# Two-chunk second and last tiles in a fused linear-attention and MLP kernel, with full-decay opening masks and a last block in halves

## The chip, the cores and the metric

The kernel runs on one core of one Trainium2 chip. The metric is the device time of one execution in microseconds (us). Profiles are of one execution; their span runs from the first to the last recorded instruction and is about 1.8 us shorter than the device time of that same execution. All runs used here are fast ones.

In the profile's lines PE is TensorE, PEld its weight loads, ACT ScalarE, DVE VectorE, POOL GpSimd and SPq the queue of SyncE. A line of a timeline gives start, duration, engine, line of the kernel, operation, what it writes `<-` what it reads, and in brackets the idle time before it with what ended it.

## The reference

Linear attention with a decay per head, then an MLP with ELU.

```python
# q, k, v: (batch 4, heads 8, seq 768, head_dim 64), lam: one decay per head
for b in range(nb):                               # blocks of the sequence
    intra = einsum('bhic,bhjc->bhij', qb, kb) * Dmask      # lam ** (i - j), causal
    intra = einsum('bhij,bhjd->bhid', intra, vb)
    inter = einsum('bhid,bhde->bhie', qb * lam_pow, kv_state)
    out[block] = intra + inter
    kv_state = lam_block * kv_state + einsum('bhsd,bhse->bhde', kb * rev_pow, vb)
x = out, as (3072 tokens, 512)
h = x @ w_in                                      # 512 x 2048
g = where(h > 0, h, exp(min(h, 0)) - 1)           # ELU
y = g @ w_out                                     # 2048 x 512
```

## The kernel before

The attention works in 24 chunks of 128 tokens (6 along the sequence for each of 4 batches, numbered with the batch fastest). The MLP works in six tiles of four chunks. A tile has 16 slices of d_ff. For a slice TensorE makes four 128x512 matmuls (`psH`, the *hidden* matmuls); ScalarE makes `e = Exp` and `r = Relu` of it; VectorE makes the ELU, `g = min(e - 1, r)`. In slices 3, 5 and 7 of tile 0 VectorE does it in two instructions instead, `m = min(e - 1, 0)` and `g = max(m, psH)`, to spare ScalarE. The *output* matmuls (`psM`) are 16 per chunk.

```python
TS = [4, 4, 4, 4, 4, 4]                           # chunks per tile
...
def mm1(t, n, alt=False):                         # one slice of a tile
    ...                                           # 4 matmuls 128x512 into pH
    nc.scalar.activation(e[:], pH[:], AF.Exp)
    if alt:
        return e, None, pH
    nc.scalar.activation(r[:], pH[:], AF.Relu)

def elu(t, n, e, r, pH):
    if r is None:
        nc.vector.tensor_scalar(out=m[:], in0=e[:], scalar1=-1.0, scalar2=0.0, op0=ALU.add, op1=ALU.min)
        nc.vector.tensor_tensor(out=gt[t][:, n, :], in0=m[:], in1=pH[:], op=ALU.max)
        return
    nc.vector.scalar_tensor_tensor(out=gt[t][:, n, :], in0=e[:], scalar=-1.0, in1=r[:], op0=ALU.add, op1=ALU.min)
```

The attention of a pair of chunks is a *visit* with three slots in the hand-written order: `s0` transposes q and k, `s1` makes the scores `psS` and their masked copy `P`, `s2` makes the outputs `psO`, the MLP input `xt` and the next state. For the pairs in the table `XT` the two transposes are DMA transposes, issued at the slot in the table; for the others TensorE transposes and ScalarE copies.

```python
XT = {12: (1, 10), 14: (2, 2), 16: (2, 10), ...}  # pair: (tile, slice) of the DMA transposes
def visit(g, s0, s1, s2):
    if g in XT:
        at(XT[g], att_xT, g)                      # nc.sync.dma_start_transpose, q then k
    else:
        at(s0, att_T, g, 2, "q"); at(s0, att_T, g, 2, "k")      # TensorE
        at(s0, att_Te, g, 2, "q", "a"); at(s0, att_Te, g, 2, "k", "a")  # ScalarE copies
    at(s0, att_kd, g, 2, "v")                     # kd = k * decay, VectorE
    at(s1, att_S, g); at(s1, att_S, g + 1); at(s1, att_mask, g); at(s1, att_mask, g + 1)
    at(s2, att_O, g, 2); at(s2, att_U, g); at(s2, att_X, g, 2); ...
for g, vs in [..., (8, ((1, 0), (1, 2), (1, 5))), (10, ((1, 8), (1, 10), (1, 13))), (12, ((2, 0), (2, 2), (2, 5))), ...]:
    visit(g, *vs)
```

All loads of q, k, v and the weights are issued by GpSimd, in a hand-written order that also holds GpSimd's two products `kd` (chunks 0 and 1, chunks 2 and 3).

Of the kernel before, what the change touches and what calls it, by code (L numbers as in the profile page):

```python
# [7 lines left out]
FP32 = mybir.dt.float32  # L8
# [7 lines left out]
def kernel(  # L16
# [10 lines left out]
    nc = tc.nc  # L27
# [9 lines left out]
    TS = [4, 4, 4, 4, 4, 4]  # L37
# [75 lines left out]
    def zero_states(e):  # L113
        for j in range(B // 2):
            for i in range(2):
                e.memset(st[j][i][:], 0.0)

    LOADS = [(0, 1, 'q'), (0, 1, 'k'), (0, 1, 'v'), (1, 1, 'q'), (1, 1, 'k'), (1, 1, 'v'), (2, 1, 'q'), (2, 1, 'k'), (3, 1, 'q'), (3, 1, 'k'), ('wi', 0), (2, 1, 'v'), ('wi', 1), (3, 1, 'v'), ('wi', 2), ('wi', 3), ('wi', 4), ('wi', 5), ('kd', 0), ('wi', 6), ('kd', 2), ('wo', 0), (4, 2), ('wo', 1), (6, 2), ('wo', 2), ('wo', 3), (8, 2), (10, 2), (12, 2), (14, 2), (16, 2), (18, 2), (20, 2), (22, 2)]
# [23 lines left out]
    rel = cpool.tile([128, 128], FP32, name="rel")  # L142
    nc.vector.tensor_copy(rel[:], rel_i[:])
    nc.vector.tensor_copy(pos[:, 0:1], rel[:, 0:1])
# [3 lines left out]
    nc.vector.tensor_scalar_add(pos[:, 1:2], pos[:, 0:1], float(L))  # L148
    nc.vector.tensor_scalar(
        out=causT[:], in0=rel[:], scalar1=0.0, scalar2=None, op0=ALU.is_ge  # L150
    )
    nc.vector.tensor_scalar(
        out=row[:], in0=rel[:], scalar1=pos[:, 0:1], scalar2=None, op0=ALU.subtract
    )

    dn = cpool.tile([128, H], FP32, name="dn")
    nc.scalar.activation(dn[:], loglam[:], AF.Exp, scale=pos[:, 0:1])
    mask = cpool.tile([128, 2, HP, 128], FP32, name="mask")
    for hh in range(2):
        nc.vector.tensor_tensor(  # L160
            out=mask[:, hh],
            in0=causT[:].unsqueeze(1).broadcast_to([128, HP, 128]),
            in1=dn[:, hh::2].unsqueeze(2).broadcast_to([128, HP, 128]),
            op=ALU.mult,
        )

    zero_states(nc.vector)
# [5 lines left out]
    def late_consts():  # L173
        for hh in range(2):
            r = slice(hh * 64, (hh + 1) * 64)
            nc.scalar.copy(loglam_p[r, :], loglam[r, hh::2])
        for hp in range(HP):
            nc.scalar.activation(
                qs[:, hp, :], row[:], AF.Exp, scale=loglam_p[:, hp : hp + 1]
            )  # L180
        nc.scalar.activation(ks[:], loglam[:], AF.Exp, scale=pos[:, 1:2])
        nc.scalar.activation(up_p[:], loglam_p[:], AF.Exp, scale=float(L))
# [75 lines left out]
    def att_mask(g, parts=1):  # L258
        P = asb.tile([128, 2, HP, 128], FP16, tag="P", name=f"P{g}", bufs=3)
        s = pS.pop(g)  # L260
        w = HP // parts
        for i in range(parts):
            c = slice(i * w, (i + 1) * w)
            nc.vector.tensor_tensor(  # L264
                out=P[:, :, c], in0=s[:, :, c], in1=mask[:, :, c], op=ALU.mult
            )
        Pt[g] = P
# [25 lines left out]
    def att_X(g, n, parts=1):  # L293
        t, i = where[g]
        if i == 0:
            xt[t] = asb.tile([128, HP, TS[t] * L], FP16, tag="xt", name=f"xt{t}")
        po = pS.pop(("O", g))
        w = HP // parts
        for j in range(parts):
            c = slice(j * w, (j + 1) * w)  # L300
            nc.vector.tensor_tensor(  # L301
                out=xt[t][:, c, i * L : (i + n) * L].rearrange("p h (n l) -> p n h l", n=n),
                in0=po[:, :, c],
                in1=qs[:, c].unsqueeze(1).broadcast_to([128, n, w, 128]),
                op=ALU.mult,
            )
# [70 lines left out]
    def mm1(t, n, alt=False):  # L377
        MT = TS[t] * L
        if (t, n) not in pH_of:
            mm1_mm(t, n, 0, MT, "M" if t == 0 and n % 2 == 1 and n < 8 else "H")  # L380
        pH = pH_of.pop((t, n))
        e = msb.tile([128, MT], FP32, tag="e", bufs=3, name=f"e{t}_{n}")
        nc.scalar.activation(e[:], pH[:], AF.Exp)  # L383
        if alt:
            return e, None, pH
        r = msb.tile([128, MT], FP16, tag="r", bufs=3, name=f"r{t}_{n}")
        nc.scalar.activation(r[:], pH[:], AF.Relu)  # L387
        return e, r, pH

    def elu(t, n, e, r, pH):  # L390
        if r is None:
            m = msb.tile([128, TS[t] * L], FP16, tag="r", bufs=3, name=f"m{t}_{n}")
            nc.vector.tensor_scalar(
                out=m[:], in0=e[:], scalar1=-1.0, scalar2=0.0, op0=ALU.add, op1=ALU.min
            )
            nc.vector.tensor_tensor(out=gt[t][:, n, :], in0=m[:], in1=pH[:], op=ALU.max)  # L396
            return
        nc.vector.scalar_tensor_tensor(  # L398
            out=gt[t][:, n, :], in0=e[:], scalar=-1.0, in1=r[:], op0=ALU.add, op1=ALU.min
        )  # L400

    def mm2(t, i, n, tag="M"):
        if n == 0:
            psM[t, i] = ps.tile([128, DM], FP32, tag=tag, bufs=2, name=f"psM{t}_{i}")
        pm = psM[t, i]
        nc.tensor.matmul(  # L406
            pm[:], lhsT=gt[t][:, n, i * L : (i + 1) * L],
            rhs=wo_t[wo_at[n][0]][:, wo_at[n][1], :], start=(n == 0), stop=(n == NF - 1),
        )
        if n < NF - 1:  # L410
            return
        c, b = divmod(T0[t] + i, B)
        t0 = b * S + c * L
        o = msb.tile([128, DM], FP32, tag="osb", bufs=3, name=f"osb{t}_{i}")
        last = T0[t] + i == NG - 1
        if last:
            hw = DM // 2
            nc.vector.tensor_copy(o[:, 0:hw], pm[:, 0:hw])
            nc.sync.dma_start(out=out[t0 : t0 + L, 0:hw], in_=o[:, 0:hw])
            nc.scalar.copy(o[:, hw:], pm[:, hw:])  # L420
            nc.scalar.dma_start(out=out[t0 : t0 + L, hw:], in_=o[:, hw:])
        else:
            if i % 2:
                nc.vector.tensor_copy(o[:], pm[:])  # L424
            else:
                nc.scalar.copy(o[:], pm[:])  # L426
            nc.sync.dma_start(out=out[t0 : t0 + L, :], in_=o[:])
        psM.pop((t, i))

    def warm(k):  # L430
        if k <= 0:
            return
        pw = ps.tile([128, 4, 128], FP32, tag="M", bufs=2, name=f"psW{len(warms)}")
        warms.append(pw)
        for _ in range(k):
            nc.tensor.matmul(
                pw[:], lhsT=ident16[:], rhs=any16, start=True, stop=True
            )
# [16 lines left out]
    def op_Te(c, w):  # L455
        att_Te(c, 1, w, "a")

    W = [5, 2, 3, 0, 1, 0, 0, 1, 1, 0, 0]
    warm(W[0])
    op_T(0, "q")  # L460
    op_Te(0, "q")
    warm(W[1])
    op_T(0, "k")
    op_Te(0, "k")
    late_consts()
# [11 lines left out]
    warm(W[5])  # L477
    op_T(2, "q")
    op_Te(2, "q")
    att_S(1)  # L480
    att_mask(1, 2)
    warm(W[6])
    op_T(2, "k")
    op_Te(2, "k")
    op_T(3, "q")
    op_Te(3, "q")
    warm(W[7])
    att_S(2)
    att_mask(2, 2)
    op_T(3, "k")  # L490
    op_Te(3, "k")
    att_O(1, 1, "M")
    att_X(1, 1)
    warm(W[8])
    att_S(3)
    att_O(2, 1, "M")
    att_X(2, 1)
    att_mask(3, 2)
    warm(W[9])
    for n in range(1):  # L500
        mm1_mm(0, n, 0, 3 * L, "HM"[n % 2])
    att_O(3, 1)
    att_X(3, 1, 2)
    warm(W[10])
    for n in range(1, 3):
        mm1_mm(0, n, 0, 3 * L, "HM"[n % 2])
    for n in range(3):
        mm1_mm(0, n, 3 * L, 4 * L)

    run_loads(LOADS[17:27])  # L510
# [8 lines left out]
    XT = {12: (1, 10), 14: (2, 2), 16: (2, 10), 18: (3, 2), 20: (3, 10), 22: (4, 2)}  # L519

    def visit(g, s0, s1, s2):
        if g in XT:
            at(XT[g], att_xT, g)
        else:
            at(s0, att_T, g, 2, "q")
            at(s0, att_T, g, 2, "k")
            at(s0, att_Te, g, 2, "q", "a")
            at(s0, att_Te, g, 2, "k", "a")
        at(s0, att_kd, g, 2, "p" if g in () else "v")
        at(s1, att_S, g)  # L530
        at(s1, att_S, g + 1)
        at(s1, att_mask, g)
        at(s1, att_mask, g + 1)
        at(s2, att_O, g, 2)
        at(s2, att_U, g)
        at(s2, att_X, g, 2)
        at(s2, att_st, g)
        at(s2, att_tmp, g + B)

    for g, vs in [(4, (('A', 11), ('A', 13), ('A', 15))), (6, (('B', 6), ('B', 9), ('B', 12))), (8, ((1, 0), (1, 2), (1, 5))), (10, ((1, 8), (1, 10), (1, 13))), (12, ((2, 0), (2, 2), (2, 5))), (14, ((2, 8), (2, 10), (2, 13))), (16, ((3, 0), (3, 2), (3, 5))), (18, ((3, 8), (3, 10), (3, 13))), (20, ((4, 0), (4, 2), (4, 5))), (22, ((4, 8), (4, 10), (4, 13)))]:  # L540
        visit(g, *vs)
    for s, a, b in [(('A', 14), 27, 28), (('A', 15), 28, 29), (('B', 11), 29, 30), (('B', 13), 30, 31), ((1, 1), 31, 32), ((1, 5), 32, 33), ((1, 9), 33, 34), ((1, 13), 34, 35)]:
        at(s, run_loads, LOADS[a:b])
# [43 lines left out]
```

## Time and profile before

Time before: 220.01 us, median of 3 runs (219.97 to 220.41); span 218.6 us.

The first lines are from the profile's page: busy time of the engines, then TensorE's busy share and clock in 40 slices of the span, the queue of the software-issued loads, and the two costliest groups.

```profile
PE 204.8 (94%) x1593; PEld 100.3 (46%) x1593; DVE 150.3 (69%) x190; ACT 126.8 (58%) x234; POOL 79.2 (36%) x76
...
PE   5979789899998999999999999999999999999992
...
PEclk9999999999999999999999999999999999999999
...
q0 software_dynamic: 80208, 13.63, 89.2%
...
L372 PE MATMUL psH<-xt,wi 128*128 128x512 f16 (+2 forms) x396 | 98.0, 372 | 2.8 <-DVE g L396 1.1
L406 PE MATMUL psM<-wo,g 128*128 128x512 f16 x384 | 97.6, 380 | 0.0
```

TensorE is the limit: it is busy 94% of the span, and after the thirteenth slice of its row (from 71 us) there are only nines until the last. The busy time by stage, in the windows view, shows where it is not.

```profile
core 0: us, PE busy (x) PEld busy (x) DVE busy (x) ACT busy (x) POOL busy (x), PEclk, DMA share, GB/s
0.00:18.00 18.00, 12.92 (x111) 6.24 (x113) 11.49 (x23) 9.49 (x20) 17.00 (x24) 1.00 1.66 121
18.00:42.00 24.00, 20.63 (x199) 10.62 (x199) 19.66 (x23) 18.85 (x35) 22.26 (x20) 1.00 1.78 183
42.00:54.00 12.00, 11.84 (x121) 6.42 (x122) 10.73 (x12) 2.67 (x4) 9.80 (x9) 1.00 2.05 173
54.00:74.00 20.00, 19.11 (x179) 9.98 (x178) 18.21 (x20) 17.14 (x31) 15.20 (x13) 1.00 2.16 175
74.00:80.00 6.00, 6.00 (x71) 3.22 (x70) 5.94 (x10) 4.35 (x10) 3.38 (x3) 1.00 2.89 154
```

From 42 to 54 us TensorE makes output matmuls of tile 0 alone, and ScalarE is busy only 2.67 of 12 us: that is what the change wants to use. Because the ends of pipelined matmuls are modelled, I also count a *stall* as the time from one matmul's start to the next, less its streaming time (columns at 216 ns for 512; small ones at their traced pace). Counted so, the stages lose 9.1, 5.1, 0.6, 1.8 and 0.1 us (the last one 74 to 78 us), and the whole span 18.3 us.

The two issued between 55 and 84 us, however, are behind the loads; the view of the tile `kT` in that window says so.

### The profile page before, as it was taken

The numbers are of one execution on the slowest core, as the hardware profiler recorded it, in microseconds if no ns is written. First come the engines' busy times: TensorE is split into PE (matmuls) and PEld (weight loads), VectorE is DVE, ScalarE is ACT, GpSimd is POOL, SyncE is SP. The second block draws the span as 40 slices with busy tenths as digits, with TensorE's granted clock in tenths as the row PEclk, the third lists the DMA queues.
The fourth block names the chain that finished last, engine by engine and source line by source line (L and its number), as shares of the span: only waits on it lengthen the run. The fifth ranks groups of instructions, "written<-read, shape, count | busy, mean of one in ns | idle before, by whom it ended". The sixth has DMA issues, their size and how long they took to land.

```text
span 218.6 us, 3968 instructions
## 1 busy us (share of the span) xinstructions
PE 204.8 (94%) x1593; PEld 100.3 (46%) x1593; DVE 150.3 (69%) x190; ACT 126.8 (58%) x234; POOL 79.2 (36%) x76
## 2 busy tenths in 40 slices
PE   5979789899998999999999999999999999999992
PEld 1444334455554544544544544545445444444440
DVE  2775879997799999897887786776666544534000
ACT  5643899332978876456466566456456566674110
POOL 8999979699958478210300000000000000000000
PEclk9999999999999999999999999999999999999999
DMA  6999999999999999999143052061011011110221
GB/s 42 144 158 190 206 163 182 183 176 157 200 184 154 157 149 167 144 166 184 39 96 97 3 116 76 2 138 58 0 48 51 0 48 48 49 51 0 96 96 49
DMA packets 96643, 23.33 MB, mean 107 GB/s; under 512 B 88816, under 2 KB 93680, under 8 KB 96624
## 3 DMA queue, kind: packets, MB, share of 16 engines
q0 software_dynamic: 80208, 13.63, 89.2%
q1 hardware_dynamic: 16272, 9.31, 18.1%
q8 instruction: 12, 0.20, 0.4%
q10 hardware_dynamic: 144, 0.13, 0.2%
q14 instruction: 7, 0.06, 0.1%
HBM read 27.27 MB, written 6.29 MB: 153 GB/s over the span
## 4 chain that ended last, share of the span: by engine, by line
PE 71%; DVE 13%; POOL 5%; ACT 5%; issue 2%; DMA 2%; DVEq 0%; POOLq 0%; ACTq 0%
PE psM L406 34%; PE psH L372 30%; DVE g L398 5%; DVE P L264 3%; PE psO L277 2%; DMA vn<-in_v_dram 2%; ACT e L383 2%; ACT r L387 2%; DVE kd L239 2%; POOL qn L72 2%; POOL kn L72 2%; PE psO L285 2%; PE psS L252 2%; POOL vn L72 1%; DVE st L355 1%
## 5 line engine op out<-in xcount | busy, mean ns | idle before, releaser
L372 PE MATMUL psH<-xt,wi 128*128 128x512 f16 (+2 forms) x396 | 98.0, 372 | 2.8 <-DVE g L396 1.1
L406 PE MATMUL psM<-wo,g 128*128 128x512 f16 x384 | 97.6, 380 | 0.0
L398 DVE SCALAR_TENSOR_TENSOR g<-e,r 128x512 f16<-128x512 f32 x93 | 71.3, 780 | 37.5 <-ACT r L387 37.3
L383 ACT ACTIVATE e<-psH 128x512 f32<-128x512 f32 x96 | 57.6, 604 | 59.3 <-PE psH L372 56.8
L372 PEld LDWEIGHTS <-wi 128*128 128x128 f16 x396 | 37.8, 98 | 47.6 <-issue 5.2
L387 ACT ACTIVATE r<-psH 128x512 f16<-128x512 f32 x93 | 55.7, 599 | 0.0
L406 PEld LDWEIGHTS <-g 128*128 128x128 f16 x384 | 36.2, 98 | 41.9
L264 DVE TENSOR_TENSOR P<-psS,mask 128x1024 f16<-128x1024 f32 (+1 forms) x28 | 28.7, 1066 | 3.1 <-PE psS L252 3.0
L336 POOL TENSOR_TENSOR tmp<-st,up_p 64x512 f32<-64x512 f16 x16 | 21.6, 1347 | 21.2 <-DVE st L355 20.3
L301 DVE TENSOR_TENSOR xt<-psO,qs 128x1024 f16<-128x1024 f32 (+2 forms) x15 | 15.0, 1008 | 7.2 <-PE psO L285 6.3
L72 POOL DMA_DIRECT2D vn<-in_v_dram x14 | 15.4, 1102 | 4.2 <-issue 4.2
L426 ACT COPY osb<-psM 128x512 f32<-128x512 f32 x12 | 7.0, 591 | 16.1 <-PE psM L406 16.1
L72 POOL DMA_DIRECT2D qn<-in_q_dram x14 | 15.7, 1124 | 1.4 <-issue 1.4
L72 POOL DMA_DIRECT2D kn<-in_k_dram x14 | 15.3, 1091 | 1.9 <-issue 1.9
L277 PE MATMUL psO<-P,vn 128*64 128x128 f16 x192 | 12.4, 223 | 1.0 <-DVE P L264 0.8
L277 PEld LDWEIGHTS <-vn 128*64 128x64 f16 x192 | 10.0, 110 | 6.3 <-issue 5.5
L424 DVE COPY osb<-psM 128x512 f32<-128x512 f32 x11 | 7.6, 689 | 5.9 <-PE psM L406 5.8
L239 DVE TENSOR_TENSOR kd<-kn,ks 128x1024 f16<-128x1024 f16 x8 | 11.5, 1443 | 0.0
L355 DVE TENSOR_TENSOR st<-tmp,psU 64x512 f16<-64x512 f32 x16 | 10.9, 680 | 0.2
L285 PE MATMUL psO<-qT,st 128*64 128x128 f16 x160 | 10.3, 219 | 0.0
L285 PEld LDWEIGHTS <-st 128*64 128x64 f16 x160 | 9.0, 110 | 0.0
L252 PE MATMUL psS<-qT,kT 64*128 64x128 f16 x192 | 8.0, 221 | 0.9 <-ACT kT L218 0.8
(44 smaller groups left out, 80.4 us busy)
## 6 DMA issues: line engine op xcount, KB each, us to landing
out_dram<-osb SPq DMA_DIRECT2D x23, 256.0 KB, 2.2
qn<-in_q_dram POOLq DMA_DIRECT2D x10, 256.0 KB, 12.6
kn<-in_k_dram POOLq DMA_DIRECT2D x10, 256.0 KB, 14.2
vn<-in_v_dram POOLq DMA_DIRECT2D x10, 256.0 KB, 13.7
wo<-in_moe_w_out_dram POOLq DMA_DIRECT2D x4, 512.0 KB, 13.2
wi<-in_moe_w_in_dram POOLq DMA_DIRECT2D x2, 512.0 KB, 8.4
wi<-in_moe_w_in_dram POOLq DMA_DIRECT2D x3, 256.0 KB, 6.1
qn<-in_q_dram POOLq DMA_DIRECT2D x4, 128.0 KB, 4.4
```

The source lines that it names most:

```text
L72: nc.gpsimd.dma_start(out=dst, in_=src[b : b + n, :, rows].rearrange("b h p d -> p (b h) d"))
L239: e.tensor_tensor(out=kd[:].rearrange("p (n h) d -> p n h d", n=n), in0=heads(kn, g, n).rearrange("p (n h) d -> p n h d", n=n), in1=ks_b, ...
L264: nc.vector.tensor_tensor(out=P[:, :, c], in0=s[:, :, c], in1=mask[:, :, c], op=ALU.mult)
L277: nc.tensor.matmul(po[r, i, hp, :], lhsT=v_of(g + i, 2 * hp + hh), rhs=P[:, hh, hp, :], start=True, stop=(c == 0), skip_group_check=True,)
L285: nc.tensor.matmul(po[r, i, hp, :], lhsT=st[(g + i) % B // 2][c % 2][:, (g + i) % 2, hp, r], rhs=qT[g + i][:, hp, :], start=False, stop=Tr ...
L301: nc.vector.tensor_tensor(out=xt[t][:, c, i * L : (i + n) * L].rearrange("p h (n l) -> p n h l", n=n), in0=po[:, :, c], in1=qs[:, c].unsqu ...
L336: e.tensor_tensor(out=tmp[r], in0=old[r, :, :, r], in1=up_p[r].unsqueeze(1).unsqueeze(3).broadcast_to([64, 2, HP, 64]), op=ALU.mult,)
L372: nc.tensor.matmul(pH[:, lo:hi], lhsT=wi[:, kk, j * 128 : (j + 1) * 128], rhs=xt[t][:, kk, lo:hi], start=(kk == 0), stop=(kk == HP - 1),)
L383: nc.scalar.activation(e[:], pH[:], AF.Exp)
L387: nc.scalar.activation(r[:], pH[:], AF.Relu)
L398: nc.vector.scalar_tensor_tensor(out=gt[t][:, n, :], in0=e[:], scalar=-1.0, in1=r[:], op0=ALU.add, op1=ALU.min)
L406: nc.tensor.matmul(pm[:], lhsT=gt[t][:, n, i * L : (i + 1) * L], rhs=wo_t[wo_at[n][0]][:, wo_at[n][1], :], start=(n == 0), stop=(n == NF - 1),
```

## The change

The intent: use idle ScalarE and VectorE time after tile 0 by making tile 1 a small tile of two chunks, which can start 10 us earlier and leaves a stock of output matmuls to fill gaps; begin tile 0 sooner by a cheaper opening; end with a small tile and the last block in two halves.

- Tiles become [4, 2, 4, 4, 4, 4, 2]. In a two-chunk tile two slices (eight matmuls 128x256) share one tile of PSUM, the memory that matmuls write, so that Exp, Relu and ELU still work on 512 columns.
- Opening: the mask for the first four chunks holds the full decay (eight Exps on ScalarE), so that their `xt` is a plain copy, mostly on ScalarE, rather than a VectorE product by `qs`. The ordinary mask is rebuilt by VectorE at slice 1 of tile 0, and two of the four state memsets move to slice 4. v of chunks 2 and 3 is loaded ahead of the first weights.
- Chunks 10 and 11 now fall at the start of a four-chunk tile and are transposed by DMA.
- The last block: two halves of 16 matmuls 128x256.

```diff
-    TS = [4, 4, 4, 4, 4, 4]
+    TS = [4, 2, 4, 4, 4, 4, 2]
...  # opening
+    def build_mask0(hh):
+        for h in range(hh, H, 2):
+            nc.scalar.activation(mask[:, hh, h // 2, :], lag[:], AF.Exp, scale=loglam[:, h : h + 1])
+        nc.vector.tensor_tensor(out=mask[:, hh], in0=mask[:, hh], in1=causT..., op=ALU.mult)
...  # att_X
+            if g < B:
+                if j == 1:
+                    nc.vector.tensor_copy(dst, po[:, :, c])
+                else:
+                    nc.scalar.copy(out=dst, in_=po[:, :, c])
+                continue
...  # mm1
+        if MT == 256:
+            pH = ps.tile([128, 2 * MT], FP32, tag="H", bufs=2, name=f"psH{t}_{n}")
+            for x in range(2):
+                for kk in range(HP):
+                    nc.tensor.matmul(pH[:, x * MT : (x + 1) * MT], lhsT=wi..., rhs=xt[t][:, kk, :], ...)
...
+    at(('A', 1), late_mask)
+    at(('A', 4), zero_state, 0, 0)
+    at(('A', 4), zero_state, 1, 0)
...
-    XT = {12: (1, 10), 14: (2, 2), 16: (2, 10), 18: (3, 2), 20: (3, 10), 22: (4, 2)}
+    XT = {10: (1, 12), 12: (2, 4), 14: (2, 12), 16: (3, 4), 18: (3, 12), 20: (4, 4), 22: (4, 12)}
...  # visits (cut)
-    (6, (('B', 6), ('B', 9), ('B', 12))), (8, ((1, 0), (1, 2), (1, 5))), (10, ((1, 8), (1, 10), (1, 13))),
+    (6, ((1, 2), (1, 4), (1, 6))), (8, ((1, 8), (1, 12), ('C', 0))), (10, ((2, 0), (2, 2), (2, 5))),
...  # order of loads, order of output matmuls, last block: cut
```

## The prediction

> **What bounds the kernel now.** Two regimes. From about 72 us the timeline shows TensorE without gaps: in the chain of waits four 128x512 matmuls take 0.86 us, 216 ns each, and 68 output matmuls in a row end the work. That is the full streaming rate (the Trainium skill, "TensorE: Matmul & The Clock Gate", section "Back-to-back issue gap", gives N/2.4 + 2.5 ns, 216 ns for 512 columns; the trace agrees). There only matmul work counts. The streams (768 wide matmuls at 216 ns = 166 us; transposes, scores, outputs, states at their traced pace, my estimate 26 us) sum to about 192 us. The last matmul ends at 214.3 us, so some 22 us are lost, all before 75 us: about 14 until tile 0's loop starts (first Exp of a hidden tile at 20.05 us), 4.4 in tile 0 (18 to 42 us), 1 in the stretch of output matmuls alone (42 to 53), 3 in tile 1. From 25 to 80 us the windows view has VectorE busy 51 of 55 us: it and ScalarE's bursts limit there.
>
> **What the change does.**
> 1. Opening. The v loads of chunks 2 and 3 go ahead of two weight loads: v3, which landed at 17.6 us and released the last psO, should land near 15.6. Four VectorE products by qs (0.69 us each) become mostly ScalarE copies (0.59); but eight 128x128 Exps (0.32 each) come in front. ScalarE is then nearly full from 5 to 17 us. The chain becomes kT3, psS, mask, psO, copy, psH: first hidden Exp at 18.2 us.
> 2. Tile 0. VectorE gets the mask rebuild (2 x 0.69), two memsets (0.49 each) and one more ELU before the masks of chunks 4 and 5. This eats most of the 1.8 us: P of chunk 5 ends at about 41 us, as before (41.05).
> 3. Tile 1 of two chunks starts its hidden matmuls at about 43.5 instead of 53.3 us; ScalarE, busy 2 of 11.4 us there, gets used. But transposes, copies (2 x 1.0), scores and masks (2 x 1.2) of chunks 6 and 7 form a serial chain with little TensorE work beside it: estimate 3 us lost (before: 1). After that 48 spare output matmuls (10 us) fill the gaps; TensorE is full from about 52 us, and tile 2, with two output matmuls per slice, does not starve. Tile 1's old loss of 3 us vanishes.
> 4. Chunk 10's transposes move to DMA: 16 x 56 ns = 0.9 us less. 256-wide matmuls cost about 0.3 us more in all.
> 5. Two-chunk last tile: the end was already matmul-bound, so nothing. The last block by halves shortens the copies after the last matmul (0.42 + 0.37, serial): 0.3 us.
>
> Sum: loss 22.3 to about 21, minus 0.9, plus 0.3, minus 0.3: about 2.5 us less; with a little for hand-chosen slots, 217.2 us. Range 214.6 to 219.4. Chances: faster by over 2% 0.24, within 2% 0.73, slower 0.03.
>
> **What would show it.** First Exp of tile 0 near 18.2 us; v3 landed before 16.5; mask of chunk 5 ending 40 to 42; first 256-wide psH at 42.5 to 44.5; TensorE gaps of about 3 us between 42 and 53, none after 55; 256-wide matmuls about 109 ns; last matmul near 212, and 4 us after it.
>
> **What would make it wrong.** Weight slices landing late now that v goes first; GpSimd's state products slowing VectorE more at the new times; VectorE not falling behind in tile 0, so that everything shifts 2 us earlier and passes 2%; 256-wide matmuls limited by weight loads; tile 2 starving behind VectorE.

## More of the kernel before

```profile
L227 SPq DMA_TRANSPOSE kT<-kn x2: 3192/4035/4878, 64.2 to 83.1; - x2
...
DMA to landing us min/median/max: 9.0/10.5/11.9
```

This is the view of the tile `kT` between 55 and 84 us. The first of the two, for chunks 12 and 13, was issued at 64.19 us and landed at 73.22. Its scores began at 82.56, so nobody waited.

From the list of DMA issues (count, median us from issue to landing): The six DMA transposes of k landed 5.2 us after issue in the median.

```profile
kT<-kn SPq DMA_TRANSPOSE x6, 5.2
```

## The result, and the profile after

The changed kernel took 222.43 us (median of 4 runs, 222.11 to 222.93) against 219.99 us for the kernel before (4 runs beside it, 219.78 to 220.41). The ratio is 1.011, with a 95% interval of 1.0085 to 1.0136. Ratios here are the mean time of one kernel's fast runs over that of the other's fast runs of the same rounds, so not quite the ratio of the medians. The prediction, 217.2 us with 214.6 to 219.4, was wrong: its direction too. The same lines of the page after:

```profile
PE 202.5 (92%) x1647; PEld 106.4 (48%) x1647; DVE 147.1 (67%) x190; ACT 129.0 (58%) x244; POOL 77.4 (35%) x76
...
PE   5867988769999699999999999999999999999992
...
PEclk9999999999999999999999999999999999999999
...
q0 software_dynamic: 80208, 13.63, 81.9%
```

After the opening TensorE's row has a 6 in the ninth slice and another in the fourteenth (each slice is 5.5 us, so 44 to 50 and 72 to 77 us). The windows view of the changed kernel, columns as before:

```profile
0.00:18.00 18.00, 12.16 (x113) 6.08 (x114) 8.54 (x19) 13.40 (x32) 17.01 (x24) 1.00 1.66 118
18.00:42.00 24.00, 19.93 (x157) 9.46 (x156) 20.46 (x26) 19.06 (x35) 18.74 (x17) 1.00 1.76 182
42.00:54.00 12.00, 9.72 (x155) 7.29 (x155) 10.47 (x13) 5.96 (x10) 8.52 (x8) 1.00 1.19 123
54.00:74.00 20.00, 19.03 (x171) 11.01 (x169) 16.04 (x19) 10.23 (x18) 16.15 (x15) 1.00 2.22 166
74.00:80.00 6.00, 4.77 (x42) 2.36 (x44) 3.85 (x5) 2.45 (x6) 1.38 (x2) 1.00 1.61 200
```

From 42 to 54 us TensorE lost 2.3 us against 0.2 before, and from 74 to 80 it is 1.2 us short where it was full; the same wait also took the last 1 us before 74. What ended it, in TensorE's timeline from 73.5 us and in the view of the tile `kT` from 55 to 80 us:

```profile
75.23 0.62 PE L263 MATMUL psS<-qT,kT 64*128 64x128 f16 x16 [2.20 <-DMA kT<-kn]
```

```profile
L238 SPq DMA_TRANSPOSE kT<-kn x2: 4246/4522/4798, 64.2 to 72.6; - x2
...
DMA to landing us min/median/max: 10.9/11.6/12.2
```

The scores of chunk 10 had to wait for its DMA-transposed k: issued at 64.24 us, landed at 75.18, wanted at about 73.0. There are 8.8 us between issue and use; the landing took 10.9.

The opening did start tile 0 sooner: v of chunk 3 landed at 15.71 us (17.58 before), and the first Exp is at 18.55 (20.05). But slice 8's Exp is at 27.62 (27.70 before), so the 1.5 us were gone eight slices later. VectorE's and GpSimd's timelines begin to show why. First VectorE's first ELU before, then the same in the changed kernel, then GpSimd's product beside it:

```profile
21.17 0.69 DVE L398 SCALAR_TENSOR_TENSOR g<-e,r 128x512 f16<-128x512 f32 x1 [2.12 <-ACT r L387]
```

```profile
19.66 2.04 DVE L433 SCALAR_TENSOR_TENSOR g<-e,r 128x512 f16<-128x512 f32 x1 [0.94 <-ACT r L420]
21.62 1.28 DVE L177 TENSOR_TENSOR mask<-causT,dn 128x512 f32<-128x512 f32 x2
```

```profile
19.22 1.92 POOL L250 TENSOR_TENSOR kd<-kn,ks 128x1024 f16<-128x1024 f16 x1
```

The ELU that took 0.69 us before takes 2.04 when it comes 1.5 us earlier, because it now starts in the middle of GpSimd's product. This agrees with the Trainium skill, "SBUF — State Buffer", section "Who interferes with whom": a VectorE instruction with two SBUF inputs contends with a GpSimd instruction that reads SBUF, and whichever came first holds the shared ports until it ends.

By stalls, as defined above, the two kernels compare so:

| stage, us | before | after | difference | what it is after |
|---|---|---|---|---|
| 0 to 18 | 9.1 | 9.3 | +0.2 | opening |
| 18 to 42 | 5.1 | 5.4 | +0.4 | wi2 late (1.24), wo0 (0.99), masked scores of chunks 4 and 5 (1.30) |
| 42 to 54 | 0.6 | 3.0 | +2.3 | tile 1: `xt` 0.65, scores of chunk 6 waiting for the copy of k 1.50 |
| 54 to 74 | 1.8 | 0.2 | −1.6 | tile 1 before, stock of output matmuls after |
| 74 to 78 | 0.1 | 2.4 | +2.3 | chunk 10's transposed k (counted at its end) |
| whole span | 18.3 | 22.0 | +3.7 | |

Fewer matmuls (16 fewer transposes, two fewer warm-ups) save about 1.0 us, so the last matmul starts 2.7 us later (216.63 against 213.93). After the end of the last matmul 4.1 us remain, 4.3 before.

### The profile page after: what moved, and what is told of

It is laid out like the page before. It is cut to its first block, busy times and chain, and to the rows that moved or that the text cites. A ratio compares the mean times of both kernels' runs of the same rounds, so it can differ in the third digit from the quotient of the medians.

```text
span 221.0 us, 4088 instructions
## 1 busy us (share of the span) xinstructions
PE 202.5 (92%) x1647; PEld 106.4 (48%) x1647; DVE 147.1 (67%) x190; ACT 129.0 (58%) x244; POOL 77.4 (35%) x76
## 4 chain that ended last, share of the span: by engine, by line
PE 73%; DVE 8%; DMA 7%; ACT 5%; POOL 3%; issue 2%; SPq 1%; POOLq 0%; ACTq 0%
PE psM L471 32%; PE psH L390 25%; PE psH L405 6%; DMA kT<-kn 5%; DVE g L433 3%; PE psS L263 3%; PE psO L289 2%; DMA qn<-in_q_dram 2%; PE psO L297 2%; DVE P L275 2%; PE psM L446 2%; ACT e L416 2%; ACT r L420 1%; POOL qn L72 1%; POOL kn L72 1%
## 5 line engine op out<-in xcount | busy, mean ns | idle before, releaser
L416 ACT ACTIVATE e<-psH 128x512 f32<-128x512 f32 x96 | 57.6, 601 | 73.5 <-PE psH L390 52.5
L433 DVE SCALAR_TENSOR_TENSOR g<-e,r 128x512 f16<-128x512 f32 x93 | 69.9, 762 | 43.1 <-ACT r L420 42.7
L471 PE MATMUL psM<-wo,g 128*128 128x512 f16 x368 | 93.7, 380 | 1.2 <-DMA wo<-in_moe_w_out_dram 1.2
L390 PE MATMUL psH<-xt,wi 128*128 128x512 f16 (+2 forms) x324 | 81.3, 376 | 1.5 <-DMA wi<-in_moe_w_in_dram 1.1
L471 PEld LDWEIGHTS <-g 128*128 128x128 f16 x368 | 34.2, 98 | 39.1 <-DMA wo<-in_moe_w_out_dram 1.3
L390 PEld LDWEIGHTS <-wi 128*128 128x128 f16 x324 | 31.3, 98 | 39.0 <-DMA wi<-in_moe_w_in_dram 1.6
L354 POOL TENSOR_TENSOR tmp<-st,up_p 64x512 f32<-64x512 f16 x16 | 19.9, 1244 | 16.6 <-DVE st L373 15.8
L405 PE MATMUL psH<-xt,wi 128*128 128x256 f16 x128 | 16.4, 273 | 0.5 <-DVE xt L320 0.5
L320 DVE TENSOR_TENSOR xt<-psO,qs 128x1024 f16<-128x1024 f32 x10 | 12.2, 1222 | 5.4 <-PE psO L297 5.2
L405 PEld LDWEIGHTS <-wi 128*128 128x128 f16 x128 | 12.4, 98 | 5.2 <-DVE xt L320 1.0
L373 DVE TENSOR_TENSOR st<-tmp,psU 64x512 f16<-64x512 f32 x16 | 10.9, 680 | 0.2
L263 PEld LDWEIGHTS <-kT 64*128 64x128 f16 x192 | 5.5, 95 | 9.9 <-ACT kT L229 4.3
```

Source lines behind the costliest of these rows:

```text
L263: nc.tensor.matmul(s[:, hh, hp, :], lhsT=kT[g][r, hp, :], rhs=qT[g][r, hp, :], start=True, stop=True,)
L320: nc.vector.tensor_tensor(out=dst, in0=po[:, :, c], in1=qs[:, c].unsqueeze(1).broadcast_to([128, n, w, 128]), op=ALU.mult,)
L354: e.tensor_tensor(out=tmp[r], in0=old[r, :, :, r], in1=up_p[r].unsqueeze(1).unsqueeze(3).broadcast_to([64, 2, HP, 64]), op=ALU.mult,)
L390: nc.tensor.matmul(pH[:, lo:hi], lhsT=wi[:, kk, j * 128 : (j + 1) * 128], rhs=xt[t][:, kk, lo:hi], start=(kk == 0), stop=(kk == HP - 1),)
L405: nc.tensor.matmul(pH[:, x * MT : (x + 1) * MT], lhsT=wi[:, kk, j * 128 : (j + 1) * 128], rhs=xt[t][:, kk, :], start=(kk == 0), stop=(kk = ...
L433: nc.vector.scalar_tensor_tensor(out=g, in0=e[:], scalar=-1.0, in1=r[:], op0=ALU.add, op1=ALU.min)
```

## The experiments

Every run below was correct. The first twelve are in sets of four. Ratios are to the kernel before in the same set, five rounds each. Where nothing else is said, an edit is made to the changed kernel. The leading theory was: **the wait for chunk 10's DMA transposes costs the time.** Its rivals: chance (the late landing of the weight slice wi2), VectorE overloaded in tile 0 by the rebuilt mask and memsets, and tile 1's serial chain.

### 1. again: the changed kernel unaltered

> The changed kernel unaltered, again, beside the kernel before on one chip. Its first trace has TensorE waiting 1.2 us at 20.4 us for the third weight slice, which landed at 20.41 us after one DMA packet of 1.5 us at 16.0 us. Theory A (a chance delay of that execution): no such packet this time, slice landed near 18.9 us, the masks of chunk 5 end a good 1 us earlier than 42.4 us. Rival B (the new load order does it each time): the same wait within 0.3 us. In both: the 2.4 us wait for the DMA-transposed keys of chunk 10 near 73 to 75 us comes back (1.5 to 3 us), and the ratio to before is 1.008 to 1.014.

Measured: 223.36 us, ratio 1.0102 (1.0067 to 1.0137). So the loss is no chance. wi2 landed at 19.08 us here (20.41 in the first trace), so its wait was chance. But the masks of chunk 5 ended only 0.34 us earlier (42.06), not a good 1 us as expected: wi2 was not what held them. The wait for k was longer: scores at 76.16 us, 3.43 us of idle. The matmuls behind it are slow; TensorE's timeline:

```profile
76.16 0.76 PE L263 MATMUL psS<-qT,kT 64*128 64x128 f16 x16 [3.43 <-DMA kT<-kn]
76.85 1.03 PE L471 MATMUL psM<-wo,g 128*128 128x512 f16 x2
77.68 1.91 PE L390 MATMUL psH<-xt,wi 128*128 128x512 f16 x4
```

Four hidden matmuls that take 1.03 us elsewhere take 1.91; start to start they are 427 ns apart rather than 216, for about 3 us. The Trainium skill, "TensorE: Matmul & The Clock Gate", section "HAM oscillation — how this bites in real kernels", warns of idle gaps of over about 3.4 us, and its section "Wait — 56ns, not 53.3ns?" gives 426.7 ns for 512 columns at the low clock. The trace agrees with the second: 427 ns. For the gaps, by the stall measure 2.36 us in the first trace left the clock at full, 3.59 here and 3.50 in mask2 below did not. But shorter stalls were followed by half clock too: 2.48 us in plus1_shift and 2.99 us in open_kd2 (runs 13 and 16), each for about 3.4 us. So the length of one gap alone does not decide it, and 3.4 us was not a safe limit here. The wait can thus cost 2.4 us or, with some eight matmuls at half speed behind it (8 x 0.21 = 1.7 us), about 5.

### 2. shift10: chunk 10's scores and outputs two slices later

```diff
-    (10, ((2, 0), (2, 2), (2, 5)))
+    (10, ((2, 0), (2, 4), (2, 7)))
```

> Only the slots of chunk 10's scores and outputs move, from slices 2 and 5 of tile 2 to slices 4 and 7. Theory: the change loses 2.4 us because the transposed keys land 9 us or more after issue (75.2 us) and the scores stand in front of them in TensorE's order; two slices later (2.6 us) they have landed, and nothing needs chunk 10 before tile 3. Expect the wait to fall under 0.5 us and the time by 1.9 to 2.5 us against the changed kernel, so about equal to before (ratio 0.999 to 1.004). Rival: VectorE is the limit there, and the wait is only moved to the outputs or to the hidden matmuls of tile 2: under 0.7 us gained.

Measured: 220.41 us, ratio 1.0006 (0.9975 to 1.0037), in the same set as the unaltered kernel's 1.0102. The wait is gone, TensorE is full again from 74 to 80 us, and the last matmul starts at 214.14 us:

```profile
74.00:80.00 6.00, 6.00 (x45) 2.67 (x45) 5.01 (x7) 4.36 (x9) 2.30 (x2) 1.00 2.00 187
```

The transposed k landed at 74.48 us, no sooner than before; it was only wanted later (75.33). So within the interval (0.3%, 0.7 us) this wait is the whole loss against the kernel before. It does not bring the predicted gain, though: 220.4, not 217.2.

### 3. open_only: the new opening with the tiles of before

The tile sizes, visits, order of output matmuls and last block of before, with the new opening.

> The new opening alone (full-decay masks, ScalarE copies, load order, late mask and state zeroing) on the tiles, slots and last block of the kernel before. Theory: the opening as such gains nothing, since the 1.5 us that the first hidden Exp comes earlier is eaten in tile 0 by late weight slices and by 2.3 us more of VectorE work: ratio 0.998 to 1.005 to before, masks of chunk 5 ending within 1 us of 41.05 us. Rival: the opening carries the loss of the change: ratio over 1.008. Second rival: the opening is the good part: ratio under 0.995.

Measured: 220.04 us, ratio 0.9975 (0.9941 to 1.0009). The opening alone gains nothing that stands out of the noise. Its first Exp was at 19.68 us in the profiled run, in which the clock stood at half until 22.0 us (0.979 over the span), and the mask of chunk 5 ended at 41.45 us (41.05 before).

### 4. mask2: the second mask in a tile of its own, built early, with all memsets in the opening

To make room, the 0/1 triangle `causT` becomes fp16; that and the memsets are cut here.

```diff
+    mask2 = cpool.tile([128, 2, HP, 128], FP32, name="mask2")
-    at(('A', 1), late_mask)
-    at(('A', 4), zero_state, 0, 0)
-    at(('A', 4), zero_state, 1, 0)
+    late_mask()          # into mask2, in the opening
```

> The changed kernel, but the second mask has a tile of its own, built in VectorE's idle time near 7 us, and all four state tiles are zeroed at 2.5 us (the 0/1 triangle is fp16 to make room). VectorE has 2.3 us less to do between 21 and 26 us. Theory VectorE-bound tile 0: masks of chunk 5 end 1 to 2 us earlier than in the unaltered run, time lower by 0.7 to 2 us. Rival DMA-bound tile 0 (second weight matrix at 30.7 us, keys of chunk 4 at 34.2 us): they end within 0.4 us of the unaltered run, time within 0.4 us.

Measured: 224.23 us, ratio 1.0176 (1.0133 to 1.0219). 2.3 us of VectorE work left tile 0, and the mask of chunk 5 still ended at 42.32 us (42.40). So taking this work away was not enough to shorten tile 0. The trial is not clean, however: in this trace TensorE's clock was at half from 18.0 to 20.8 us (0.50 in the windows view), which the unaltered kernel's traces do not have; run 17, at full clock, takes this work away and more, and its mask of chunk 5 ended at 41.84. In the profiled execution chunk 10's wait was 3.3 us and the clock fell behind it; that this makes the run the slower one is likely, but no run tests it.

### 5. loads_late: loads of chunks 12 to 23 issued later

```diff
-    ((1, 8), 29, 30), ((1, 12), 30, 31), (('C', 1), 31, 32), (('C', 4), 32, 33), ((2, 1), 33, 34), ((2, 5), 34, 35)
+    (('C', 0), 29, 30), (('C', 4), 30, 31), ((2, 1), 31, 32), ((2, 4), 32, 33), ((2, 7), 33, 34), ((2, 10), 34, 35)
```

> The changed kernel with the loads of chunks 12 to 23 issued later (chunk 12's after tile 1 instead of in its middle, the others behind it), everything else as it was, the scores of chunk 10 still in slice 2. Theory: the transposes of chunk 10 took 10 to 11 us because the software loads of chunks 12 and 14 sit in the same 16 DMA engines; with these held back they take 3 to 6 us, land before 70 us, and TensorE's wait (2.4 and 3.6 us in the two traces) falls under 0.5 us: 2 to 3.5 us faster than the changed kernel, ratio to before 0.995 to 1.003. Rival: a DMA transpose takes about 10 us whatever else is queued: wait stays over 2 us. Risk: chunk 12's own transposes now come too late and the wait reappears there.

Measured: 222.83 us, ratio 1.011 (1.0075 to 1.0146). The view of the tile `kT` from 55 to 80 us:

```profile
L238 SPq DMA_TRANSPOSE kT<-kn x2: 1321/1981/2641, 63.1 to 77.6; - x2
...
DMA to landing us min/median/max: 3.2/6.0/8.9
```

With fewer loads in flight chunk 10's k was transposed in 3.2 us (63.11 to 66.30) instead of 10.9, and its wait is gone. So the transposes are slow because they share with the loads. That is as the Trainium skill has it ("DMA: Bandwidth & Descriptors", section "Issuing engines are not separate DMA queues": DMAs of all issuing engines run on the same 16 DMA engines and interleave). But the loads that moved now lie on the next transposes: waits of 1.58 us at 86.54 us (chunk 12) and 0.57 at 116.1 (chunk 14). The gain was given back.

### 6. x10_pe: chunk 10 transposed by TensorE

```diff
-    XT = {10: (1, 12), 12: (2, 4), ...
+    XT = {12: (2, 4), ...
```

> The changed kernel with chunk 10 and 11 transposed by TensorE and copied by ScalarE as in the kernel before, in slice 0 of tile 2, scores still in slice 2. This costs 16 transposes (0.9 us of TensorE) and two copies of 1.0 us on ScalarE. If the DMA transposes are the cause of the loss: wait for the keys under 1 us, 1.3 to 2.6 us faster than the changed kernel, ratio to before 0.999 to 1.006, so slower than the kernel with the scores moved. If the loss sits elsewhere in tile 2: within 0.7 us of the changed kernel.

Measured: 221.11 us, ratio 1.0038 (1.0000 to 1.0077). The wait is gone here too. Undoing this one line removes most of the loss.

### 7. fill_shift: shift10, and output matmuls moved into tile 1's chain

The output matmuls after tile 0 are taken earlier: eight instead of four in the first slot, then four in each slot of tile 1's chain.

> The kernel with chunk 10's scores moved (220.4 us, ratio 1.0006), and besides the output matmuls of tile 0 that the change keeps for slices 8 to 14 of tile 1 and after are spread one to two slots earlier, so that TensorE has work while it waits for the x tile of chunk 4 and for the keys of chunks 6 and 7 (waits of 0.64 and 1.50 us). Same instructions, other order. Theory: the short tile 1 opened a serial chain with too little TensorE work beside it, worth 1.5 to 2.1 us: expect 1.0 to 2.0 us less, ratio 0.991 to 0.997. Rival: TensorE is not what sets the end of that chain (VectorE or ScalarE is), the waits come back at other places: under 0.5 us.

Measured: 220.17 us, ratio 0.9997 (0.9962 to 1.0031). No gain over shift10: a new wait of 1.68 us at 45.44 us, output matmuls on the weights wo2, which had not landed.

### 8. old_last_shift: shift10 with the last block of before

> The kernel with chunk 10's scores moved, but with the last output block as in the kernel before: 16 matmuls of 512 columns, then two copies of 256 columns. Tells what the last block by halves is worth: 0.1 to 0.4 us slower than the kernel with the scores moved (ratio to before 1.001 to 1.003) by shorter copies after the last matmul; if 256-wide matmuls at 114 ns cost more than the copies save, equal or faster.

Measured: 220.54 us, ratio 1.0012 (0.9971 to 1.0052), against shift10's 1.0006 in another set: the last block by halves is worth too little to see. The comparison is not clean: in the profiled execution the k of chunk 10 landed at 75.93 us, and the wait came back with 1.2 us. Two slices of distance are barely enough.

### 9. noalt_shift: shift10, slices 3, 5, 7 of tile 0 with Relu on ScalarE

```diff
-    er = mm1(t, n, alt=t == 0 and n in (3, 5, 7))
+    er = mm1(t, n, alt=False)
```

> The kernel with chunk 10's scores moved, and in tile 0 slices 3, 5 and 7 use ScalarE's Relu like the others instead of VectorE's add-and-min from SBUF. Reason: in every trace so far that VectorE operation ends 0.24 to 0.27 us after GpSimd ends issuing a load (24.44 after 24.18, 27.48 after 27.23, 28.62 after 28.38), and the first ELU ends at 21.70 us in all runs with the new opening, 0.56 us after GpSimd's product; the Exp of slice 8 starts at 27.6 us in all of them, however early the first Exp is (18.55 to 20.05). Theory: GpSimd's timetable, which the new opening doesn't move, holds tile 0; without those three operations the Exp of slice 8 starts at 26.3 to 27.0 us, and TensorE's wait at 25.2 us is gone. Whether time falls: if the loads (second weight matrix, keys of chunk 4) hold the later half, the masks of chunk 5 still end at 41.4 to 42.4 us and the time stays within 0.5 us of 220.4; else up to 1 us less. Rival: ScalarE or the weight slices hold slice 8: its Exp stays at 27.6 us or comes later.

Measured: 220.89 us, ratio 1.0049 (1.0009 to 1.0088). Slice 8's Exp did not move (27.84 us). The first Exp was late in this trace (19.54 us), and the clock was at half from 18.0 to 20.8 us (0.50 in the windows view), so it decides nothing.

### 10 to 12. fill2_shift, kdlate_shift, both_shift: three ways to shorten tile 1's chain

fill2_shift is a milder fill_shift. kdlate_shift moves VectorE's product `kd` of chunks 4 and 5 behind the masks of chunks 4 and 5 (`at((1, 0), att_kd, 4, 2)`). both_shift does both.

> As the run that spread the output matmuls earlier, which gained nothing because at 45.4 us TensorE met output matmuls of slice 8 whose weights had not landed (1.68 us wait) ahead of tile 1's hidden matmuls. Here the ones of slices 8 and 9 stand behind the transposes of chunk 6 (47.5 us), so the weights are there, and the rest one slot earlier each. Theory: TensorE's 1.50 us wait for the keys of chunk 6 falls to about 0.6 us and nothing comes back: 0.7 to 1.1 us less than the kernel with the scores moved (ratio 0.995 to 0.998). Rival: gained time is given back later (tile 2 then waits for its x tile or for ScalarE): under 0.4 us.

> The kernel with chunk 10's scores moved, and the k product of chunks 4 and 5 (2.06 us on VectorE, in front of their masks) and what hangs on it (state update) moved behind their x product, one slot later. Theory: in the end of tile 0 VectorE stands between TensorE and tile 1 (waits of 1.3 and 0.7 us for the masks and 0.64 us for x at 40 to 45 us): masks of chunk 5 end 1 to 2 us earlier (39.5 to 41.0), the first 256-wide matmuls start 1.5 to 2.2 us earlier (42 to 42.8 us), time 0.7 to 2 us less than 220.4. Rival: the masks wait for ScalarE's copies and the keys' landing (34 us) instead, or VectorE pays the product back before the masks of chunks 6 and 7: under 0.5 us.

> The scores of chunk 10 moved, the output matmuls respread as above and the k product moved, together. If the two theories hold and are independent, 1.4 to 3 us under 220.4 us, so faster than the kernel before by 0.5 to 1.2%. If only one holds, its gain alone.

Measured: 220.94, 220.65 and 220.77 us, ratios 1.0048 (1.0011 to 1.0086), 1.0035 (0.9997 to 1.0074) and 1.0061 (1.0017 to 1.0104). Each shortened the wait that it aimed at, and each met another one close behind. fill2_shift cut the wait of chunk 6's scores from 1.50 to 0.64 us and got 0.93 at 58.7 us (a buffer of the output matmuls, which a ScalarE copy freed late). kdlate_shift ended the mask of chunk 5 at 41.13 us (41.41 in shift10), and that of chunk 7 at 52.52 instead of 51.62.

### 13 to 16. What holds slice 8 of tile 0?

In all twelve runs slice 8's Exp came at 27.6 to 28.3 us, whatever the opening. Four runs shift GpSimd's timetable. plus1_shift puts four small GpSimd instructions (iota) ahead of the product of chunks 2 and 3; kd2later_shift moves that product behind the loads of chunk 4; kd2noalt_shift also takes the alternate slices away; open_kd2 has the tiles of before, the new opening, the new last block and the moved product.

```diff
-    ('wi', 6), ('kd', 2), ('wo', 0), (4, 2), ('wo', 1), ...
+    ('wi', 6), ('iota', 4), ('kd', 2), ('wo', 0), (4, 2), ('wo', 1), ...    # plus1_shift
+    ('wi', 6), ('wo', 0), (4, 2), ('kd', 2), ('wo', 1), ...                 # kd2later_shift
```

> Chunk 10's visit moved as in shift10, and four extra small GpSimd instructions (about 0.9 us) ahead of GpSimd's product of chunks 2 and 3. If GpSimd's timetable holds slice 8: the first ELU ends near 22.6 us (21.7 in the first run), the Exp of slice 8 comes at 28.4 to 28.7 us (27.6). Rival (ScalarE or the weights hold it): slice 8 stays at 27.6. Time: 220.4 to 221.4 us, ratio 1.000 to 1.006 either way, so the time alone does not decide.

> As shift10, with GpSimd's product of chunks 2 and 3 moved behind chunk 4's loads. If GpSimd's timetable holds slice 8: the first ELU takes 0.7 us instead of 2.0 and ends near 20.4 to 20.8 us, the Exp of slice 8 comes at 26.3 to 27.2 us (27.6), and the time is up to 1 us less than shift10's (ratio 0.995 to 1.001), less if a later load binds. Rival: slice 8 stays at 27.6 and the ratio at 1.000.

> As kd2later_shift, and slices 3, 5 and 7 of tile 0 get their Relu on ScalarE like the others. If both VectorE's alternate slices and GpSimd's product held slice 8: its Exp at 26.3 to 27.0 us. If ScalarE is the limit: at 27.5 or later (eight slices with two ScalarE instructions each). Time: ratio 0.995 to 1.002.

> Tiles of the kernel before, with the new opening, the last block by halves, and GpSimd's product of chunks 2 and 3 moved behind chunk 4's loads; no two-chunk tiles. open_only measured 0.9975. If GpSimd's timetable held slice 8 and TensorE waits on it: ratio 0.990 to 0.997. If not: 0.996 to 1.000.

| run | us | ratio | slice 8's Exp, us |
|---|---|---|---|
| plus1_shift | 221.74 | 1.0062 (1.0020 to 1.0105) | 30.33 |
| kd2later_shift | 222.81 | 1.0122 (1.0073 to 1.0171) | 32.54 |
| kd2noalt_shift | 221.42 | 1.0076 (1.0031 to 1.0122) | 29.45 |
| open_kd2 | 221.53 | 1.0063 (1.0019 to 1.0107) | 30.96 |

The leading forecasts of all four missed. Slice 8 did move, so GpSimd's timetable can delay it; that does not yet show what holds it at 27.6 us. Moving the product later, which should have helped, hurt most. VectorE's timeline of kd2later_shift, then GpSimd's, then TensorE's:

```profile
23.46 3.03 DVE L433 SCALAR_TENSOR_TENSOR g<-e,r 128x512 f16<-128x512 f32 x2
26.41 1.07 DVE L428 TENSOR_SCALAR m<-e 128x512 f16<-128x512 f32 x1
```

```profile
23.37 1.96 POOL L250 TENSOR_TENSOR kd<-kn,ks 128x1024 f16<-128x1024 f16 x1
```

```profile
28.26 1.01 PE L390 MATMUL psH<-xt,wi 128*128 128x512 f16 x2 [4.02 <-DVE g L431]
```

The product now falls on the ELUs of slices 1 and 2, when VectorE already has a queue: two ELUs take 3.03 us instead of 1.28, and TensorE waits 4.02 us for VectorE. In plus1_shift the product fell on the mask's rebuilding (two instructions, 2.99 us; 1.28 in the changed kernel). The times in the table are not the collision's alone: behind it TensorE's clock fell to half in three of the four (plus1_shift from 26.7 to 30.1 us, kd2later_shift from 26.8 to 33.6, open_kd2 from 27.0 to 30.4; 0.50 in the windows view of plus1_shift from 26.75 to 30 us). plus1_shift also shows what does not collide: its first ELU ran for the most part beside iotas, which only write, and took 0.69 us. One thing stays open. In kd2later_shift, kd2noalt_shift and open_kd2 the first ELU took 2.12, 1.75 and 1.50 us with only load issues on GpSimd. The other ELUs beside load issues took 0.62 to 0.69.

### 17 and 18. m2noalt_shift and m2noaltvec_shift: the suspected VectorE work taken away together

m2noalt_shift has shift10, the early second mask and memsets of mask2, and no alternate slices. m2noaltvec_shift also gives the product of chunks 2 and 3 to VectorE, before the first ELU.

```diff
-    ('wi', 6), ('kd', 2), ('wo', 0), ...
+    ('wi', 6), ('wo', 0), ...
+    att_kd(2, 2, "v")                             # m2noaltvec_shift
```

> Chunk 10's visit moved, the late mask built early in a tile of its own with the state memsets (as mask2), and slices 3, 5, 7 of tile 0 on ScalarE (as noalt_shift): VectorE has no TENSOR_SCALAR, mask or memset left between slices 0 and 8. If VectorE's queue holds slice 8: its Exp moves from 27.6 to 26.5 to 27.2 us in a run whose wi2 lands by 20.4 us. Rival (one of these alone was never the limit, the weights are): 27.6 or later. Time: ratio 0.994 to 1.002; less than 1 us is expected, so the time alone decides little.

> As m2noalt_shift, and the product of chunks 2 and 3 made by VectorE before the first ELU instead of by GpSimd, so that GpSimd issues the loads about 1.9 us earlier. If GpSimd's product is what made the first ELU late: that ELU takes 0.7 us (2.0 in the first run) and ends by 21.0 us; Exp of slice 8 at 26.3 to 27.0 us. Rival: slice 8 stays at 27.6 or later. Time: ratio 0.992 to 1.002.

Measured: 220.33 us, ratio 1.0001 (0.9955 to 1.0048), and 220.49 us, ratio 1.0009 (0.9967 to 1.0051). In m2noalt_shift slice 8's Exp came at 26.58 us, as expected: VectorE's work in tile 0 is what held it (27.61 to 27.64 us in the six traces in which that work was unaltered and the clock full). Whether one half alone would move it stays open: mask2 (27.61) and noalt_shift (27.84) did not, but both had half the clock at the start of tile 0. In m2noaltvec_shift the first ELU took 0.69 us and ended at 20.51, as expected, so GpSimd's product had made it late. Slice 8's Exp came at 27.35, later than expected: TensorE waited 0.35 us at 23.76 and 0.41 at 26.27, where wi4 and wi5 had just landed (23.72 and 26.23; 22.29 and 25.02 in m2noalt_shift).

Why does 1 us at slice 8 change nothing at the end? In the list of waits of m2noalt_shift from 28 to 35 us, TensorE's are:

```profile
PE psM L476 <- DMA wo<-in_moe_w_out_dram: 1.3, 1, 1.3
...
PE psT L222 <- DMA kn<-in_k_dram: 0.5, 1, 0.5
```

At 30.16 us the first output matmul waits for wo0, and at 33.88 the transposes wait for k of chunk 4 (landed at 33.83; 33.18 in the kernel before). Whatever tile 0 gains before 30 us is spent waiting for loads. The mask of chunk 5 ended at 41.84.

No version beat the kernel before clearly. The best ratios are 0.9975 (open_only), 0.9997 and 1.0001, with intervals that hold 1.

Two things were left untested. The small tiles were never run with the opening of before, so their own share, with the last block, is only the difference between shift10 and open_only, whose intervals overlap. And the results give each execution's mean clock: 0.995 to 0.999 as a set's average for the kernel before, 0.983 to 0.998 for the changed kernel in the eighteen runs. In eight of the nineteen traces with the new opening (shift10's is one) the clock fell back to half for 3.4 to 6.8 us between 15 and 22 us; the kernel before's trace has no such stretch. What this costs, no run separates.

## Why the prediction was wrong

The step that failed is the end of point 3: "After that 48 spare output matmuls (10 us) fill the gaps; TensorE is full from about 52 us, and tile 2, with two output matmuls per slice, does not starve." TensorE starved after the hidden matmuls of slice 2 of tile 2, from 73.0 to 75.2 us. The prediction booked chunk 10's move to DMA, in its point 4, as 0.9 us less work for TensorE, and nowhere asked when the transposes would land. The page gave a median of 5.2 us for them, but the first pair in the trace of before had taken 7.9 (q) and 9.0 us (k), at about the time when chunk 10's would be issued. Spare output matmuls did not help: in the program they stand behind the scores, and in the trace none of them ran during the wait.

Term by term, in us of difference to the kernel before:

| term of the sum | predicted | measured |
|---|---|---|
| opening and tile 0, to 42 us | about 0 | +0.6 |
| 42 to 54 us | +2 (3 instead of 1) | +2.3 (3.0 instead of 0.6) |
| tile 1's old loss, 54 to 74 us | −3 | −1.6 |
| tile 2's start | 0 | +2.3, more when the clock falls |
| matmul work (transposes, 256-wide) | −0.6 | −1.0, with the warm-ups |
| after the last matmul | −0.3 | −0.2 |
| sum | −1.9 (the record's own sum gives −2.2, calls it about −2.5, and its 217.2 us is −2.8) | +2.4 (spans: +2.4) |

- Opening: right in kind. First Exp 18.55 us (18.2 predicted), v of chunk 3 at 15.71 (15.6 predicted).
- Tile 0: the text said that extra VectorE work eats most of the 1.8 us. It does (m2noalt_shift), with GpSimd's product on top. Without it the head start is lost to loads of wo0 and k of chunk 4, which the prediction did not see. The mask of chunk 5 ended at 42.40 us (42.06 in the repeat), not 41.
- Start of tile 1: the first 256-wide hidden matmul came at 44.80 us (42.5 to 44.5 predicted; 44.46 in the repeat), and the gaps from 42 to 54 us were 3.0 us (3 predicted). Right within 0.3 us.
- "Tile 1's old loss of 3 us vanishes": it vanished, but it was 1.8 us in all, of which 1.6 went. This term was mis-sized by 1.4 us.
- 256-wide matmuls: eight in 0.87 us, 109 ns each, as predicted; weight loads did not limit them.
- The warning "tile 2 starving behind VectorE" named the place but not the cause.

Two amounts close the account. shift10 shows that without chunk 10's wait the change is worth nothing that can be seen (1.0006, interval 0.9975 to 1.0037). The other part of the missing gain is in the mis-sized terms: 1.4 us of tile 1, 0.6 of the opening and tile 0, and 0.3 from 42 to 54 us. That these three add up is arithmetic on single traces, not shown by runs of their own.

## What to carry to other kernels

Before work moves from an engine to a DMA, compare the distance between issue and use with the landing time of such a DMA at that moment under its load, not with the median of the page; here 8.8 us of distance met 10.9 us of landing, in a kernel whose median was 5.2. A stock of other work does not cover such a wait if it stands behind it in the engine's program. And a head start is worth only what the next resource can take: here it went first to VectorE behind GpSimd, and once that was removed, to weights that had not landed.

## What the Trainium skill lacked or had wrong

- Landing time of a small SBUF-to-SBUF DMA transpose beside other DMAs ("DMA: Bandwidth & Descriptors" says that they share the engines, but gives no landing time): 3.2 us with few loads in flight (loads_late), 9.0 to 12.2 us with the software-issued loads of the same stage (the k transposes issued from 64 to 84 us in the first two traces).
- "SBUF — State Buffer", section "Who interferes with whom", was right for the GpSimd product (an ELU took 2.04 us instead of 0.69) and for an iota (0.69). It names `tensor_scalar` among the operations that can contend with GpSimd, but gives no size for VectorE beside GpSimd's *issuing of loads*: TENSOR_SCALAR took 0.42 us with GpSimd idle (kd2later_shift, 31.40 us) and anything from 0.41 to 1.19 beside load issues. The two-input ELU mostly took 0.62 to 0.69 beside them, but the first ELU of tile 0 took 1.50 to 2.12 us in three runs, which the section does not explain.
- "TensorE: Matmul & The Clock Gate" was right about the low clock: 427 ns per 512 columns. Its warning, idle gaps of over about 3.4 us, is no safe limit: half clock followed stalls of 3.59 and 3.50 us, but also of 2.48 us (plus1_shift) and 2.99 us (open_kd2), while 2.36 us left the clock at full.
